# The second MoE's first product as fifteen block products on a Trainium2 core, with an order from a list scheduler

## The chip, the core and the metric

The kernel runs on one core of a Trainium2 chip. The metric is device time in microseconds (us) of one execution, and the median of three runs stands for the kernel. All weights, activations and results are float32. A product is made exact enough by splitting each operand in a high part of reduced precision (`hi`) and the rest (`lo`) and adding three TensorE products: hi·hi, hi·lo and lo·hi.

The engines are named as the profile names them: PE is TensorE's matmul stream and PEld its weight loads, DVE is VectorE, ACT is ScalarE, POOL is GpSimd, and SP is SyncE, whose queue issues every DMA of this kernel. PSUM has 8 banks of 128x512 float32. TensorE writes only there, and DVE or ACT must read a bank out before it can be filled anew.

## What is computed

Three stages follow each other; the output of one is the input of the next.

```
attention:  state = f[t] * state + k[t] v[t]^T ;  y[t] = q[t] . state      (4 x 8 heads, 768 steps, 48 wide)
first MoE:  h = x @ w_in ;  g = h * sigmoid(1.702 h) ;  x = g @ w_out      (3072 tokens, 384 -> 2048 -> 384)
second MoE: p = domain_probs / sum(domain_probs)
            out = sum over e of  p[:, e] * (relu(x @ w1[e]) @ w2[e])       (4 experts, 384 -> 1024 -> 384)
```

The change concerns `x @ w1[e]` and all that follows from computing it in another way.

## The kernel before

Activations lie transposed in SBUF: features on the 128 partitions, 512 tokens in a row. 3072 tokens make six token tiles `j` (NB = 6), 384 features make three partition tiles (KD = 3).

**Attention and first MoE.** Two parts of the program carry them. `startup` runs an order that is written out as a table (`ORDER`), with all attention of the first two token tiles and 40 steps of the first MoE. The steps after that are 64 steps of 512 tokens (16 blocks of hidden features for each of the token tiles 2 to 5). A step `s` has a product into a bank (L538, nine matmuls), a tanh on ACT (L544), a multiplication on DVE that reads the bank (L546), the split into hi on ACT (L326) and lo on DVE or POOL (L328), and, two steps later, the second product (L556, nine matmuls, into three banks). `at` and `chunk_at` hang the attention of the chunks 12 to 23 between the first 48 of these 64 steps; the framework's own scheduler orders that part, under the engines' in-order queues. The last 16 steps stand in written order.

**Second MoE.** The weights are eight units `u` (two for each expert), each with a 384x512 block of `w1` and a 512x384 block of `w2`. The loop runs over u, j and four blocks `ft` of 128 hidden features. `L3` makes the first product: three parts of the precision scheme times three feature tiles, nine matmuls of 512 columns into bank 3 or 4 (L626); DVE takes the relu and multiplies by the token's probability (L633), then ACT and DVE split the result. `L4`, two steps behind, makes the second product, nine matmuls into three of six banks (L664), and after four `ft` DVE adds the three banks to an accumulator in `arena` (L675). The last unit's last token tile is computed with tokens on the partitions (`L4_last`, L697, 384 columns) so that no transpose stands at the end. `at` places the loads and splits of the next unit's weights among the steps. POOL has no work in this stage.

For each unit and pair of token tiles the first product so takes 3 x 3 x 4 x 2 = 72 matmuls: per 256 hidden features and three token tiles, 2 x 3 blocks of output with three 128-wide inner products each are 18 block products of three matmuls.

**Names.** `R` are twenty 128x1536 tiles (the first MoE's weights and inputs, later the second MoE's), `G` eight split results, `RAW` (`cv` in the profile) six 128x512 tiles that `raw_tile` hands out in turn, `WIDE` three 128x1024 tiles, `ydram` the first MoE's output in DRAM, `ptd` the probabilities there.

## Time and profile before

| | us |
|---|---|
| median of 3 runs (1318.56, 1320.10, 1320.69) | 1320.1 |
| span of the profiled execution, first to last instruction | 1318.0 |
| span from the first product of the second MoE to its last matmul | 787.7 |
| PE busy in the span | 1287.3 |
| DVE, ACT, POOL busy | 734.9, 385.4, 167.6 |

The profiled execution has no time of its own besides its span; the median is 2.1 us longer than that span, which is what lies around the first and the last instruction and the spread of the runs.

The profile is read in four views. The page gives the busy time of each engine and the chain that ended last. The view of windows gives the same busy times, the granted clock of TensorE (1.00 is the upper of its two levels, 2.4 GHz) and the DMA engines' busy share for stretches that one names. The view of groups by line gives count, busy time and mean duration. The timeline gives single instructions, with the idle time before them and what ended it in brackets.

### The profile page before, as it was taken

Reading aid. Unit: us, or ns where it says so; the run is one execution under the profiler, and the core shown is the slowest. Engines: PE = TensorE matmul, PEld = TensorE weight load, DVE = VectorE, ACT = ScalarE, POOL = GpSimd, SP = SyncE. Lnnn points to the kernel's source line nnn. Section 1 sums busy time; section 2 is a strip of 40 time slices with the busy share of each in tenths; the row PEclk is TensorE's granted clock in tenths of the full one; section 3 lists DMA queues with packets and bytes.
Section 4 is the critical chain, followed back from the end, with each engine's and each line's share of the span. In section 5 each row is a group of like instructions: output and inputs, shape, how many; then the busy total and the mean of one; then the engine's idle time right before and its main releaser. Section 6 shows DMA issues by size and latency. Waiting matters only on the chain.

```text
span 1318.0 us, 18850 instructions
## 1 busy us (share of the span) xinstructions
PE 1287.3 (98%) x7734; PEld 1069.2 (81%) x7734; DVE 734.9 (56%) x1111; ACT 385.4 (29%) x691; POOL 167.6 (13%) x179
## 2 busy tenths in 40 slices
PE   5799999999999999999999999999999999999998
PEld 4698887888888888888888888888888888888887
DVE  7889747666565354455454454454454454454554
ACT  4666634333333343222121121121121121121111
POOL 5877422111110022000000000000000000000000
PEclk6899999999999999999999999999999999999999
DMA  6554323112120042420100100100100100100353
GB/s 181 171 157 135 100 73 105 42 52 77 27 71 21 7 139 89 120 80 33 48 25 24 48 24 25 48 25 25 48 25 24 49 24 24 48 25 16 48 97 75
DMA packets 75040, 81.63 MB, mean 62 GB/s; under 512 B 43104, under 2 KB 44224, under 8 KB 74944
## 3 DMA queue, kind: packets, MB, share of 16 engines
q1 hardware_dynamic: 74944, 80.34, 21.6%
q8 instruction: 62, 1.02, 0.3%
q14 instruction: 34, 0.28, 0.1%
HBM read 66.90 MB, written 13.42 MB: 61 GB/s over the span
## 4 chain that ended last, share of the span: by engine, by line
PE 95%; POOL 2%; DMA 1%; ACT 1%; issue 1%; DVE 0%; SPq 0%; POOLq 0%; ACTq 0%
PE bank L626 30%; PE bank L664 29%; PE bank L538 15%; PE bank L556 15%; PE bank L496 2%; PE bank L428 2%; PE bank L422 1%; PE bank L697 1%; DMA wide<-in_w_in 1%; POOL cv L87 0%; PE bank L457 0%; POOL arena L441 0%; POOL arena L419 0%; DMA arena<-in_qkf 0%; POOL g L328 0%
## 5 line engine op out<-in xcount | busy, mean ns | idle before, releaser
L626 PE MATMUL bank<-r,r 128*128 128x512 f32 x1728 | 423.0, 390 | 0.0
L664 PE MATMUL bank<-g,r 128*128 128x512 f32 x1692 | 414.1, 390 | 0.0
L626 PEld LDWEIGHTS bank<-r,r 128*128 128x128 f32 x1728 | 324.5, 188 | 67.1
L664 PEld LDWEIGHTS bank<-g,r 128*128 128x128 f32 x1692 | 317.8, 188 | 65.7
L326 ACT CAST g<-wide 128x512 fp32r<-128x512 f32 x192 | 119.3, 621 | 633.0 <-DVE wide L633 633.0
L633 DVE SCALAR_TENSOR_TENSOR wide<-bank,wide 128x512 f32<-128x512 f32 x192 | 132.6, 691 | 244.9 <-PE bank L626 244.5
L538 PE MATMUL bank<-r,r 128*128 128x512 f32 (+1 forms) x936 | 219.7, 380 | 2.9 <-DVE arena L546 2.1
L556 PE MATMUL bank<-g,r 128*128 128x512 f32 (+1 forms) x936 | 215.9, 375 | 0.0
L328 DVE TENSOR_TENSOR g<-wide,g 128x512 fp32r<-128x512 f32 x192 | 132.9, 692 | 142.9 <-ACT g L326 142.9
L538 PEld LDWEIGHTS bank<-r,r 128*128 128x128 f32 x936 | 165.4, 190 | 36.3 <-DVE arena L546 2.3
L556 PEld LDWEIGHTS bank<-g,r 128*128 128x128 f32 x936 | 166.5, 188 | 32.7 <-DVE cv L565 0.7
L546 DVE SCALAR_TENSOR_TENSOR arena<-arena,bank 128x512 f32<-128x512 f32 (+1 forms) x104 | 66.0, 636 | 88.3 <-ACT arena L544 88.0
L544 ACT ACTIVATE arena<-bank 128x512 f32<-128x512 f32 (+1 forms) x104 | 58.7, 564 | 129.8 <-PE bank L538 129.3
L328 DVE TENSOR_TENSOR g<-arena,g 128x512 fp32r<-128x512 f32 (+1 forms) x82 | 60.4, 736 | 37.9 <-ACT g L326 37.8
L326 ACT CAST g<-arena 128x512 fp32r<-128x512 f32 (+1 forms) x104 | 61.0, 588 | 69.6 <-DVE arena L546 69.4
L675 DVE TENSOR_TENSOR arena<-arena,bank 128x512 f32<-128x512 f32 x123 | 77.4, 678 | 0.0
L326 ACT CAST r<-cv 128x512 fp32r<-128x512 f32 x84 | 51.4, 616 | 4.8 <-POOL cv L87 3.5
L328 DVE TENSOR_TENSOR r<-cv,r 128x512 fp32r<-128x512 f32 x70 | 49.0, 704 | 0.5 <-ACT r L326 0.4
L428 PE MATMUL bank<-arena 48*128 48x128 f32 x384 | 30.8, 304 | 12.5 <-issue 5.9
L428 PEld LDWEIGHTS bank<-arena 48*128 48x128 f32 x384 | 25.8, 205 | 17.4 <-issue 9.6
L412 DVE TENSOR_TENSOR_SCAN arena<-arena,ends 128x512 f32<-128x512 f32 x24 | 35.5, 1481 | 0.2
L406 DVE TENSOR_TENSOR_SCAN arena<-arena,floor 128x512 f32<-128x512 f32 x24 | 31.7, 1320 | 1.7 <-POOL s_dec L470 0.4
(79 smaller groups left out, 623.5 us busy)
## 6 DMA issues: line engine op xcount, KB each, us to landing
wide<-ptd SPq DMA_DIRECT2D x48, 256.0 KB, 3.6
cv<-in_w SPq DMA_DIRECT2D x42, 256.0 KB, 4.0
arena<-in_qkf SPq DMA_DIRECT2D x48, 192.0 KB, 3.5
ydram<-cv SPq DMA_DIRECT2D x30, 256.0 KB, 2.2
cv<-ydram SPq DMA_DIRECT2D x30, 256.0 KB, 3.5
arena<-in_v SPq DMA_DIRECT2D x24, 256.0 KB, 3.5
wide<-in_w_in SPq DMA_DIRECT2D x12, 512.0 KB, 4.5
wide<-in_w_out SPq DMA_DIRECT2D x12, 512.0 KB, 3.9
```

What stands on the lines that cost most here:

```text
L326: nc.scalar.copy(out=hi, in_=src)
L328: eng.tensor_tensor(out=lo, in0=src, in1=hi.bitcast(F32), op=ALU.subtract)
L412: nc.vector.tensor_tensor_scan(back, back, ends[:, ::-1], 0.0, ALU.mult, ALU.max)
L428: nc.tensor.matmul(ab(c)[1 + r][:, 128 * p:128 * p + 128], t[64 * r:64 * r + D, 1, p], t[64 * r:64 * r + D, 2, p], start=True, stop=True,)
L538: nc.tensor.matmul(h, w[:, c0:c0 + 128], x[:, 512 * k + t0:512 * k + t0 + n], start=(i == 0), stop=(i == 8),)
L544: nc.scalar.activation(out=th, in_=h, func=ACTF.Tanh, scale=0.851)
L546: nc.vector.scalar_tensor_tensor(out=gf, in0=th, scalar=1.0, in1=h, op0=ALU.add, op1=ALU.mult)
L556: nc.tensor.matmul(bank[d][:, t0:t0 + n], w[:, c0:c0 + 128], g, start=(f == fs[0] and i == 0 and t0 == 0), stop=(f == fs[-1] and i == 2 an ...
L626: nc.tensor.matmul(h, w[:, c0:c0 + 128], y[:, 512 * k:512 * k + 512], start=(i == 0), stop=(i == 8),)
L633: nc.vector.scalar_tensor_tensor(out=gf, in0=h, scalar=0.0, in1=wide(NB * u + j, 0), op0=ALU.max, op1=ALU.mult)
L664: nc.tensor.matmul(cur[d], w[:, c0:c0 + 128], h, start=(ft == 0 and s == 0), stop=(ft == 3 and s == 2),)
L675: nc.vector.tensor_tensor(out=a, in0=a, in1=cur[d], op=ALU.add)
```

## The change

The three weight blocks of 128 input features by two halves of 256 hidden features, and the three token tiles, are treated as a product of a 2x3 by a 3x3 matrix of blocks. Instead of the 18 block products of the ordinary rule, the new kernel computes 15 products of sums of blocks, from which the six output blocks follow exactly by additions (`FORM_W`, `FORM_Y`, `FORM_H`: which blocks are summed on the weight side, on the token side, and where a product enters).

- `w_forms`, `w2_piece`: in the 48 steps of the first MoE between which attention hangs, each unit's `w1` is loaded, POOL makes 12 sums of blocks (128x256), ACT and DVE split 15 forms into hi and lo, and SP stores them in DRAM (`wfd`, 15 x 256 KB for each unit). `w2` is split too and stored (`w2d`). The six `RAW` tiles carry all of it.
- `second_moe` builds a list of tasks with engine, an assumed duration and the buffers that they read and write; `Plan.order` puts them into an order, engine by engine, always taking the task that can begin first. TensorE's own order is fixed by a number for each task (`place`). The list begins with the last 16 steps of the first MoE (`l_task`, `m_task`) and the token side's first forms.
- 32 rounds `n` follow, one for each half unit of 256 hidden features and each half of the tokens (three token tiles). A round has 15 products of three matmuls (`p_task`, L1076) in five chains; a chain's products add up in one bank, and after each product ACT or DVE reads the running sum out (L1089, L1093), so that the next product of that chain waits for that read. Relu and split follow on ACT (L1100) and DVE (L1101). Then come nine second products of six matmuls (`u_task`, L1116), each read by DVE with the probability (L1129) and added to the accumulator by POOL (L1131). The last two rounds use 12 products of 384 columns (`u_last`, L1166).
- The token side's 15 forms of the second half are made on POOL during the rounds 2 to 12 (`later_forms`), kept in DRAM (`yfd`) and split in rounds 14 and 15. The first half's output leaves after round 15.

```diff
-    def L3(u, j, ft):
-        for w, y in ((whi, yhi), (whi, ylo), (wlo, yhi)):
-            for k in range(KD):
-                nc.tensor.matmul(h, w[:, c0:c0 + 128], y[:, 512 * k:512 * k + 512], start=(i == 0), stop=(i == 8))
-        nc.vector.scalar_tensor_tensor(
-            out=gf, in0=h, scalar=0.0, in1=wide(NB * u + j, 0), op0=ALU.max, op1=ALU.mult
-        )
...
+CHAINS = [[3, 8, 14, 11, 12, 0], [13, 7, 10, 6, 1], [2], [5], [4, 9]]
+TURN = [3, 13, 8, 7, 2, 14, 5, 10, 11, 4, 6, 9, 12, 1, 0]
+U_START = 17.0
...
+        def form(r):
+            def go():
...
+                        nc.gpsimd.tensor_tensor(
+                            out=t, in0=have[a], in1=have[b], op=ALU.add if sg > 0 else ALU.subtract
+                        )
...
+                hl = raw_tile().rearrange("p (i l c) -> p i l c", i=2, l=2)
...
+                    nc.scalar.copy(out=hi, in_=fv)
+                    nc.vector.tensor_tensor(out=lo, in0=fv, in1=hl[:, :, 0], op=ALU.subtract)
...
+                nc.sync.dma_start(
+                    out=wfd[2 * u:2 * u + 2, g, :, 256 * q:256 * q + 256].rearrange("i p c -> p i c"),
...
+        def dma(nbytes, fns, reads=(), writes=(), after=()):
...
+            return P.task("SP", 0.1 * max(1, nbytes // 262144), go, reads, writes, after, late=2.2 + nbytes / 220e3)
...
+            P.task("POOL", pool, lambda: nc.gpsimd.tensor_tensor(
+                out=a.ap, in0=a.ap, in1=m.ap, op=ALU.add), [a, m], [a])
...
+        plan = second_moe()
+        done = plan.order()
         with tc.manual_schedule():
-            first_steps(e, len(steps) - early)
...
+            for t in done:
+                t.fn()
```

How the instructions stand now is shown at three places. The first is PE's queue in the second MoE. Before, a step of the first product (L626) and one of the second (L664) alternate, nine matmuls each; `bank` is the PSUM bank, after the arrow stand the streamed operand and the weights.

```order
L626 MATMUL bank3_98<-r2_65,r14_77 128x512 x3
L626 MATMUL bank3_98<-r3_66,r14_77 128x512 x3
L626 MATMUL bank3_98<-r2_65,r15_78 128x512 x3
L664 MATMUL bank5_100<-g4_87,r18_81 128x512
L664 MATMUL bank6_101<-g4_87,r18_81 128x512
L664 MATMUL bank7_102<-g4_87,r18_81 128x512
L664 MATMUL bank5_100<-g5_88,r18_81 128x512
L664 MATMUL bank6_101<-g5_88,r18_81 128x512
L664 MATMUL bank7_102<-g5_88,r18_81 128x512
```

Now, at the end of round 10, products of three matmuls (L1076) stand between second products of six (L1116):

```order
L1076 MATMUL bank6_101<-r9_72,r13_76 128x512 x3
L1076 MATMUL bank5_100<-r3_66,r13_76 128x512 x3
L1116 MATMUL bank0_95<-r14_77,r7_70 128x512
L1116 MATMUL bank0_95<-g3_86,r7_70 128x512
L1116 MATMUL bank0_95<-r14_77,r7_70 128x512
L1116 MATMUL bank0_95<-g5_88,r7_70 128x512
L1116 MATMUL bank0_95<-r14_77,r7_70 128x512
L1116 MATMUL bank0_95<-g3_86,r7_70 128x512
L1076 MATMUL bank6_101<-r10_73,r13_76 128x512
L1076 MATMUL bank6_101<-r11_74,r13_76 128x512
L1076 MATMUL bank6_101<-r10_73,r13_76 128x512
```

Bank 6 is filled, must be read out, and is filled again with three plus six matmuls in between.

The second place is DVE's queue in the same stage. Before, it alternates between the relu that reads a bank (L633) and the split (L328), with three additions (L675) every four steps:

```order
L675 TENSOR_TENSOR arena_91<-arena_91,bank5_100 128x512
L675 TENSOR_TENSOR arena_91<-arena_91,bank6_101 128x512
L675 TENSOR_TENSOR arena_91<-arena_91,bank7_102 128x512
L633 SCALAR_TENSOR_TENSOR wide0_92<-bank3_98,wide2_94 128x512
L328 TENSOR_TENSOR g5_88<-wide0_92,g4_87 128x512
L633 SCALAR_TENSOR_TENSOR wide1_93<-bank4_99,wide2_94 128x512
L328 TENSOR_TENSOR g7_90<-wide1_93,g6_89 128x512
```

Now, in round 10, with the read of bank 6 that the PE rows above wait for in the sixth row:

```order
L1093 TENSOR_TENSOR arena_91<-arena_91,bank5_100 128x512
L1129 TENSOR_TENSOR arena_91<-bank2_97,cv01_123 128x512
L1093 TENSOR_TENSOR arena_91<-arena_91,bank4_99 128x512
L1129 TENSOR_TENSOR arena_91<-bank1_96,cv02_124 128x512
L1101 SCALAR_TENSOR_TENSOR r19_82<-arena_91,g7_90 128x512
L1093 TENSOR_TENSOR arena_91<-arena_91,bank6_101 128x512
L1093 TENSOR_TENSOR wide0_92<-wide0_92,bank5_100 128x512
L1129 TENSOR_TENSOR arena_91<-bank0_95,cv02_124 128x512
L1101 SCALAR_TENSOR_TENSOR g0_83<-arena_91,r19_82 128x512
```

The reads of banks now stand behind splits (L1101) that read two operands from SBUF.

The third place is SP's queue in the first MoE. Before, it holds the loads of attention (L386, L388) and every sixteen steps three stores of results (L571):

```order
L388 DMA arena_91<-in_v 128x512
L386 DMA arena_91<-in_qkf 48x512 x2
L571 DMA ydram_106<-cv01_120 128x512
L571 DMA ydram_106<-cv02_121 128x512
L571 DMA ydram_106<-cv10_122 128x512
L386 DMA arena_91<-in_qkf 48x512 x2
L386 DMA arena_91<-in_qkf 48x1024 x2
```

Now the stores of the forms (L794), the loads of `w2` (L807) and the stores of its halves (L810, L811) stand between the same loads (L527, L529):

```order
L527 DMA arena_91<-in_qkf 48x512
L794 DMA wfd_109<-cv00_122 128x2x256
L794 DMA wfd_109<-cv10_125 128x2x256
L807 DMA cv11_126<-in_w2 128x512
L527 DMA arena_91<-in_qkf 48x1024 x2
L810 DMA w2d_110<-cv12_127 128x512
L811 DMA w2d_110<-cv11_126 128x512
L794 DMA wfd_109<-cv10_125 128x2x256
L807 DMA cv02_124<-in_w2 128x512
L529 DMA arena_91<-in_v 128x512
```

208 DMAs have come into this part of the queue: 16 loads of `w1`, 24 of `w2`, 120 stores of forms and 48 of the halves of `w2`.

## Rows read from the trace of the kernel before

**Rows 1.** The page: busy time by engine, and the chain that ended last.

```profile
PE 1287.3 (98%) x7734; PEld 1069.2 (81%) x7734; DVE 734.9 (56%) x1111; ACT 385.4 (29%) x691; POOL 167.6 (13%) x179
...
PE 95%; POOL 2%; DMA 1%; ACT 1%; issue 1%; DVE 0%; SPq 0%; POOLq 0%; ACTq 0%
```

**Rows 2.** Windows: stretch, length, busy us, PEclk, DMA share, GB/s.

```profile
182.00:456.00 274.00, 273.88 (x2453) 223.19 (x2453) 160.98 (x251) 101.12 (x185) 38.43 (x56) 1.00 0.19 55
100.00:140.00 40.00, 40.00 (x254) 33.84 (x253) 37.22 (x49) 27.54 (x52) 28.48 (x22) 1.00 0.42 130
523.80:1311.50 787.70, 787.70 (x3487) 653.95 (x3485) 396.50 (x602) 149.74 (x251) 0.00 (x0) 1.00 0.16 42
```

**Rows 3.** PE's timeline, second MoE's start and end: start, span, instruction.

```profile
531.95 2.20 PE L626 MATMUL bank<-r,r 128*128 128x512 f32 x9
...
536.03 2.20 PE L626 MATMUL bank<-r,r 128*128 128x512 f32 x9
...
1301.03 2.27 PE L697 MATMUL bank<-r,g 128*128 128x384 f32 x12
1303.13 2.24 PE L626 MATMUL bank<-r,r 128*128 128x512 f32 x9
```

**Rows 4.** Groups by line, PE, whole span: count, busy us, mean ns.

```profile
L626 PE MATMUL bank<-r,r 128*128 128x512 f32 x1728 | 423.0, 390 | 0.0
L664 PE MATMUL bank<-g,r 128*128 128x512 f32 x1692 | 414.1, 390 | 0.0
...
L697 PE MATMUL bank<-r,g 128*128 128x384 f32 x48 | 8.7, 336 | 0.0
```

**Rows 5.** Groups by line and form: DVE from 182 to 456 us.

```profile
L328 DVE TENSOR_TENSOR g<-arena,g 128x512 fp32r<-128x512 f32 x51 | 36.9, 724 | 24.8 <-ACT g L326 24.8
...
L412 DVE TENSOR_TENSOR_SCAN arena<-arena,ends 128x512 f32<-128x512 f32 x14 | 21.1, 1507 | 0.1
...
L406 DVE TENSOR_TENSOR_SCAN arena<-arena,floor 128x512 f32<-128x512 f32 x14 | 17.1, 1225 | 1.1
```

**Rows 6.** The same view, DVE and POOL, whole span.

```profile
L546 DVE SCALAR_TENSOR_TENSOR arena<-arena,bank 128x256 f32<-128x256 f32 x16 | 6.4, 408 | 2.5 <-ACT arena L544 2.5
...
L342 POOL TENSOR_TENSOR cv<-cv,cv 128x512 f32<-128x512 f32 x12 | 16.7, 1390 | 71.0 <-DMA cv<-ydram 70.6
...
L328 POOL TENSOR_TENSOR g<-arena,g 128x256 fp32r<-128x256 f32 x10 | 10.5, 1053 | 3.0 <-ACT g L326 3.0
```

**Rows 7.** Timeline of POOL and DVE around 329 and 75 us.

```profile
328.94 1.80 POOL L419 TENSOR_TENSOR arena<-arena 128x512 f32<-128x512 f32 x1 [7.36 <-DMA arena<-in_qkf]
329.51 1.79 DVE L328 TENSOR_TENSOR g<-arena,g 128x512 fp32r<-128x512 f32 x1
...
74.90 0.72 POOL L328 TENSOR_TENSOR g<-arena,g 128x256 fp32r<-128x256 f32 x1
```

**Rows 8.** DMA: two windows of 5 us, then issues with KB and us to landing.

```profile
180.00:185.00 5.00, 5.00 (x54) 3.89 (x53) 3.89 (x9) 2.90 (x7) 1.80 (x2) 1.00 0.66 213
535.00:540.00 5.00, 5.00 (x24) 4.14 (x23) 1.68 (x3) 1.21 (x2) 0.00 (x0) 1.00 0.94 268
...
ydram<-cv SPq DMA_DIRECT2D x30, 256.0 KB, 2.2
```

**Rows 9.** Timeline of one step of the first MoE.

```profile
332.90 2.20 PE L538 MATMUL bank<-r,r 128*128 128x512 f32 x9
...
335.20 0.60 ACT L544 ACTIVATE arena<-bank 128x512 f32<-128x512 f32 x1 [2.10 <-PE bank L538]
...
337.21 0.69 DVE L328 TENSOR_TENSOR g<-arena,g 128x512 fp32r<-128x512 f32 x1 [0.69 <-ACT g L326]
```

**Rows 10.** SP's queue: waits from 182 to 456 us, then two timeline rows.

```profile
SPq L386 <- PE bank L496: 120.6, 10, 17.6
...
194.93 1.31 SPq L571 DMA_DIRECT2D ydram<-cv  x3
1284.33 7.05 SPq L646 DMA_DIRECT2D out<-cv  x12
```

More of the change, by code (lines that the diff above doesn't have):

```diff
@@ new lines, with __init__, ap, at @@
+U_TOKENS = [2, 1, 0]
+U_START = 17.0
+LAST_U = 30
+class Buf:
+    def __init__(self, pool, parts=None):
+        self.pool, self.slot = pool, None
+        self.writers, self.readers, self.refs = [], [], []
+    @property
+    def ap(self):
+        return self.slot.ap
+class Slot:
+    def __init__(self, ap, free=0.0):
+        self.ap, self.held, self.free = ap, None, free
+    def at(self):
+        if self.held is None:
+            return self.free
+        if any(t.end is None for t in self.held.refs):
+            return None
+        return max([self.free] + [t.end + t.late for t in self.held.refs])
@@ L278, in attention_moe_moe2_kernel @@
     ptd = dram.tile([4, NT], F32, name="ptd")
-    otd = dram.tile([512, DM], F32, name="otd")
+    yfd = dram.tile([15, 128, 512], F32, name="yfd")
+    wfd = dram.tile([2 * NU, 5, 128, 768], F32, name="wfd")
+    w2d = dram.tile([NU, 2, 128, 1536], F32, name="w2d")
+    otd = dram.tile([NT // 2, DM], F32, name="otd")
     yrows = [[i for i, g in enumerate(SEGS) if g[0] == j] for j in range(2)]
@@ L359, in attention_moe_moe2_kernel @@
     last = NB - 1
-    ys = [wout[0], win[1], wout[1], win[2], wout[2], win[3]]
-    us = [(xs[1 - last % 2], win[0]), (wout[3], xs[last % 2])]
     def eng(kind, i):
@@ L585, in L2, with slot, asl @@
             sums_store(row, tiles)
-    onum = [0]
-    obanks = [5, 6, 7, 0, 1, 2]
-    def wide(i, n):
-        return WIDE[i % 3].bitcast(F32)[:, 512 * n:512 * n + 512]
+    def slot(i):
+        return [*(WIDE[n // 2].bitcast(F32)[:, 512 * (n % 2):512 * (n % 2) + 512] for n in range(6)),
+                *RAW, ends, floor][i]
+    def asl(i):
+        return arena[:, 512 * i:512 * i + 512]
     def pr_make():
@@ L679, in attention_moe_moe2_kernel @@
[L679 to L705 removed]
+    place_of = {r: i for i, r in enumerate(TURN)}
@@ L775, in startup @@
                 step(int(ev[1:]), ev[0])
+    e_last = len(steps) - early - 16
     if True:
@@ L797, in attention_moe_moe2_kernel @@
                 chunk_at(4 * j + 4 + i, max(0, 16 * (j - 2) + 4 * i - 2))
[L799 to L838 removed]
+        e = len(steps) - early - 16
+        at(e - 8, pr_make)
+        when = [i for i in range(1, e - 1) if i % 16 not in (0, 1)]
+        work = []
+        for u in range(NU):
+            load, forms = w_forms(u)
+            pieces = [w2_piece(u, n) for n in range(3)]
+            work.append([load])
+            for i in range(5):
+                work.append(forms[3 * i:3 * i + 3] + (pieces[i // 2:i // 2 + 1] if i % 2 == 0 else []))
+        for i, fns in enumerate(work):
+            for fn in fns:
+                at(when[i * len(when) // len(work)], fn)
+        for i in range(e):
+            for fn in side.pop(i, []):
+                fn()
+            L1(early + i)
+            if len(pend) > 2:
+                L2()
         nc.vector.tensor_reduce(
```

637 lines of the change are left out of this document (491 added, 146 removed), and 8 rows, old and new, of tables (FORM_H, FORM_Y).

## The prediction

> **What bounds the kernel now.** I read the page first: PE is busy 98% of the span, and the chain that ended last is PE for 95% of it [rows 1]. A busy PE is not yet a PE at its peak, so the windows come next: from 523.8 to 1311.5 us PE never idles, its granted clock is 1.00, and POOL does nothing [rows 2]. The timeline then gives the pace: two steps of nine matmuls take 536.03 - 531.95 = 4.08 us, 0.2267 us for a matmul of 512 columns [rows 3], for a step that fills one bank and one that changes banks at every matmul alike. The groups give the counts [rows 4]: 1728 + 1692 matmuls of 512 columns at 0.2267 are 775.3 us, and 48 of 384 columns at (1303.13 - 1301.03) / 12 = 0.175 are 8.4, together 783.7. With the 18 matmuls of the first MoE that lie in the same stretch (4.1) this is the 787.7 of the window. So the second MoE is bound by the number of its matmuls alone, and a matmul less is worth 0.2267 us as long as nothing else makes PE wait.
>
> The stretch from 182 to 456 us, where the new work on weights goes, is bound by PE in the same way, but its cover is thinner: PE 273.9 of 274, DVE 161.0, ACT 101.1, POOL 38.4, DMA share 0.19 [rows 2].
>
> **Matmuls, the gain.** The new order holds 1440 matmuls at L1076, 1620 at L1116 and 144 of 384 columns at L1166. That is 3060 x 0.2267 + 144 x 0.175 = 693.7 + 25.2 = 718.9 us against 783.7: 64.8 us less. The shapes are the old ones (128x128 weights, 512 columns), so the pace is taken over. That the fifteen products are really fifteen the order shows (32 rounds x 15 x 3 = 1440); the rival that the change does not do what it says is closed. The profiled execution spans 1318.0 us, the median is 1320.1; I add the 2.1 between them to every result, so with no new wait the median is 1318.0 - 64.8 + 2.1 = 1255.3.
>
> **First MoE's stretch, the largest cost.** Eight units bring 120 forms, 96 sums and 24 pieces of w2 into 274 us in which PE has no slack. Each resource in turn.
>
> DVE: 120 splits of 128x256. The nearest row, 128x256 with one operand in PSUM, is 0.408 [rows 6]: 49 us, so 210 of 274. ACT: 120 halves of 128x256 at less than the 0.60 of a 128x512 [rows 9] and 24 pieces at that are below 87 us, so 188 of 274. POOL: 96 sums at 0.72 (undisturbed [rows 7]) to 1.05 (mean [rows 6]) and 24 subtractions at 1.39 [rows 6] are 102 to 134, so 141 to 172 of 274.
>
> DVE and POOL are not independent. At 328.94 a POOL operation took 1.80 us, and beside it a DVE split of two SBUF operands took 1.79 [rows 7] instead of 0.69 [rows 9]. DVE's splits and scans with two SBUF operands in this stretch take 75 us now [rows 5], 124 with the new ones; with POOL's 141 they ask for 265 of 274 us if no part of them overlaps. In SBUF — State Buffer, section "SBUF: two separate sides", the Trainium skill says that DVE with two SBUF inputs and GpSimd take one port pair as a lock for the whole instruction: then nothing overlaps, which speaks against this change and is the mechanism of rival (b). The two rows at 329 us agree with it in kind; but from 100 to 140 us DVE and POOL were busy 37.2 and 28.5 of 40 us and PE lost nothing [rows 2].
>
> DMA: 6.3 MB of w1 and 6.3 of w2 are read, 12.6 of w2's halves and 31.5 of forms are written, 56.6 MB. Loads reached 268 GB/s at a share of 0.94 (285 if full); a window with three stores 213 at 0.66 (323 if full) [rows 8]. At the full rates the new traffic takes 44 + 137 = 181 us, if stores keep their pace with 1 KB rows, and 56.6 MB at 268 GB/s are 211; with the old 0.19 x 274 = 52 it is 233 to 263 of 274. In DMA: Bandwidth & Descriptors, section "Specifications", the Trainium skill gives about 358 GB/s as the HBM limit of a core; by that estimate the new traffic is 158 us, this item is slack, and of the 15 us below some 5 would go. No window here comes near that rate, so the measured one decides.
>
> So DVE, DMA and the pair stand at 77 to 97% of the stretch and none above 100%. Every queue is in order: an ACT cast that waits for one of six `cv` tiles, a store or a POOL sum holds the tanh behind it. What hides such a wait: a step's second product begins 4 x 2.04 = 8.2 us after its first has ended, and the chain of tanh, product and split takes 337.21 + 0.69 - 334.94 = 3.0 us [rows 9], so about 5 us of delay in one step cost nothing. The bounds: 0, since nothing exceeds the window (a gain is excluded, PE's work there is the same); and 265 / 0.85 - 274 = 38 if in-order queues fill the pair, or DMA, to 85% only. I take **15**, nearer to the row from 100 to 140, but not 0, because DMA stood at 0.42 there and stands near 0.9 here.
>
> **Hand-over, 16 steps.** At its head SP issues 21 loads of results, three of probabilities and the first weights, in the plan 0.1 us apart and landing 3.4 us later, so the last of the 21 after 6. The trace shows 1.31 / 3 = 0.44 us for an issue [rows 10] and 256 KB at 268 GB/s are 1 us, so it lands after about 25. Twelve POOL sums and eight DVE sums wait for these loads, and DVE's multiplications of the running steps (L877) stand behind. Between 0 (5 us are free in each step, and the first form is due only after 16 x 4.08 = 65 us) and 25 - 6 - 5 = 14; I take **3**.
>
> **Steady rounds.** A round is 99 x 0.2267 = 22.4 us of PE. DVE has 24 operations of 0.69, 16.6 us, POOL nine additions of 1.39 (the nearest row [rows 6]), 12.5, and ACT 11 of 0.6. Five splits of a round have two SBUF operands and meet POOL's additions half the time, which adds 5 x 0.5 x 0.7 = 1.7 to DVE: 18.3 of 22.4. The closest place is the bank-6 pair in the order: between its end and its next filling PE has 3 + 6 matmuls, 2.04 us. The read begins 335.20 - 334.94 = 0.26 after the end [rows 9], takes 0.69, and stands behind a split that on its own ends in time: about 0.9 us are spare. A POOL addition just begun holds that split for up to 1.39, which costs at most 0.5 once a round, 16 in 31 rounds, and at least 0; in the middle, where an addition is often not just begun, about 0.13 a round: **4**.
>
> **The turn at half and the end.** After round 15, 36 stores in 128-byte pieces leave. Twelve such stores kept SP for 7.05 us [rows 10], so 36 take 21 of the round's 22.4 us, and weights for the next round queue behind, which are asked for more than ten microseconds ahead. 0 to 8, I take **2**. The tail after the last matmul has the old form; 0.
>
> **Sum.** 1255.3 + 15 + 3 + 4 + 2 = 1279.3, say **1280**.
>
> **Rivals.** (a) All is hidden in the stretch. For it: each resource has room on average, and 100 to 140 us shows full queues without loss. Then only hand-over, rounds and turn cost up to 9: 1255 to 1265. (b) The port pair and DMA fill to 85% only, 38 us, and the rounds pay 10 rather than 4: 1255.3 + 38 + 3 + 10 + 2 = 1308, with 1298 to 1317 around it. For it: three loaded in-order queues that wait for each other; against it: the row from 100 to 140. (c) Slower: SP's one queue. Attention's loads hold it while they wait for PE, 120.6 us in ten waits, the longest 17.6 [rows 10]. Nothing urgent stands behind them today. Then 208 DMAs do, and while a load holds the queue no store leaves, the six `cv` tiles fill up, and ACT stops with its tanh. Price: 284 issues (76 are there before) at 0.44 are 125 us, the holds 121, and 24 loads of w2 that wait for the landing of their tile's last store (2.2 us [rows 8]) 53: 299, 25 more than the stretch. It makes the kernel slower once the sum passes 274 + 65 = 339, that is if the holds grow by 40 us; with 60 more it is 1255.3 + 85 + 9 = 1349. Against it: the order puts the loads among the stores, not ahead of them, so much of the holding should go.
>
> **How the numbers follow.** Forecast (stretch 5 to 30, 1266 to 1298): 0.55. (a): 0.20. (b): 0.16. Within the noise: 0.02. (c): 0.07. The range leaves out (c), the upper part of (b) and the lowest of (a): 1257 to 1311. About 0.2% (2.6 us) is what a measurement of this kernel can tell from no change. Faster by more 0.91, within 0.02, slower 0.07.
>
> **What will show it.** The gain: groups at L1076, L1116 and L1166 with 1440, 1620 and 144 matmuls, and 4.08 us for 18 in the rounds. The stretch: the time from the first cast of a form (L786) to the last of the 48 steps, 274 before, and PE's idle time there, put down to L679 or L697 behind ACT or DVE, with DMA shares near 0.9. Rival (c): SP's waits for PE, with casts that wait for stores. The rounds: PE idle at L1076 behind DVE L1093. Wrong would be a pace over 0.2267 us with a PE that never idles, or over 50 us of idle PE in the rounds. If PE idles for long at a time its clock may fall too, which my sum does not contain.

## The result, and the profile of the changed kernel

The changed kernel takes 1339.0 us, the kernel before 1320.4 (medians of four runs each, side by side): 1.015 times as long, 95% interval 1.0135 to 1.0166. I had forecast 1280. The profiled execution spans 1337.5 us; by the matmuls that are gone it should span 1318.0 - 64.8 = 1253.2, so 84.3 us were lost on the way.

The page of the changed kernel, busy time by engine and the chain that ended last (beside [rows 1]):

```profile
PE 1249.2 (93%) x7470; PEld 1026.9 (77%) x7470; DVE 975.6 (73%) x1443; ACT 515.5 (39%) x967; POOL 691.2 (52%) x591
...
PE 66%; DVE 11%; DMA 10%; issue 5%; POOL 5%; ACT 2%; SPq 1%; DVEq 0%; ACTq 0%; POOLq 0%
```

PE is busy for 38 us less, not 65, and it is 66% of the chain instead of 95%.

Groups by line, PE, whole span, and its timeline in a round (beside [rows 3, 4]):

```profile
L1076 PE MATMUL bank<-r,r 128*128 128x512 f32 x1440 | 376.9, 391 | 9.9 <-DVE arena L1093 8.2 <-DVE wide L1093 1.1 <-ACT arena L1089 0.3
L1116 PE MATMUL bank<-r,r 128*128 128x512 f32 x876 | 273.9, 389 | 0.0
L1116 PE MATMUL bank<-g,r 128*128 128x512 f32 x744 | 242.9, 389 | 0.0
```

```profile
701.06 1.52 PE L1076 MATMUL bank<-r,r 128*128 128x512 f32 x6
...
705.14 0.61 PE L1116 MATMUL bank<-g,r 128*128 128x512 f32 x2
```

The counts are those of the sum (L1166 has its 144 in two further groups, 76 and 68), and 6 + 2 + 2 + 2 + 6 = 18 matmuls take 705.14 - 701.06 = 4.08 us, as before. The gain of 64.8 us is there.

Where the 84 us went, by windows (length, busy us, PEclk, DMA share, GB/s). The borders are the first matmul of step 49, where the last sixteen steps of the first MoE begin (L869, 515.9 us), and the first matmul of the second MoE (L1076, 592.6):

```profile
182.00:515.90 333.90, 292.51 (x2433) 232.38 (x2433) 231.64 (x376) 151.59 (x331) 148.74 (x170) 0.95 0.67 212
515.90:592.60 76.70, 70.01 (x290) 55.37 (x289) 51.41 (x63) 27.57 (x49) 30.98 (x21) 0.96 0.41 144
605.00:936.00 331.00, 330.90 (x1457) 273.31 (x1458) 250.42 (x359) 102.63 (x170) 196.69 (x139) 1.00 0.52 166
936.00:990.00 54.00, 49.80 (x212) 38.95 (x211) 48.75 (x73) 19.07 (x33) 21.87 (x15) 1.00 0.78 188
990.00:1285.00 295.00, 295.00 (x1303) 244.21 (x1302) 220.60 (x321) 87.94 (x144) 161.38 (x115) 1.00 0.44 133
1285.00:1296.00 11.00, 5.79 (x19) 4.31 (x18) 5.89 (x9) 2.42 (x4) 2.27 (x2) 0.69 0.69 130
```

The same two stages before:

```profile
182.00:458.40 276.40, 276.28 (x2465) 225.08 (x2465) 161.67 (x252) 102.27 (x187) 38.43 (x56) 1.00 0.19 55
458.40:523.80 65.40, 65.40 (x292) 54.20 (x291) 30.86 (x45) 26.89 (x48) 16.68 (x12) 1.00 0.36 118
```

- The stretch with the work on weights: step 49 begins at 515.9 instead of 458.4, **57.5 us**. PE is idle for 333.9 - 292.5 = 41.4 of them, and the same work keeps it busy for 292.5 instead of 276.3 us, some 16 more, at a granted clock of 0.95 instead of 1.00.
- The hand-over: 76.7 - 65.4 = **11.3**.
- In the rounds PE is idle for 0.1 us from 605 to 936 and not at all from 990 to 1285. The turn at half and the end of round 29 lose 6 and 7 (each matmul's start against the pace of 0.2267), the first round 1.3.

57.5 + 11.3 + 1.3 + 6 + 7 is 83; the rest lies at the start and in the tail.

**How one pause comes about.** The longest in the stretch, before 383.9, in the timeline of all engines (start, length, instruction; in brackets the idle time before it and what ended it):

```profile
364.68 0.56 SPq L758 DMA_DIRECT2D wide<-in_w  x1
...
369.83 2.31 POOL L777 TENSOR_TENSOR wide<-wide 128x256 f32<-128x256 f32 x3 [6.88 <-DMA wide<-in_w]
...
377.99 0.62 POOL L538 TENSOR_SCALAR arena<-arena 128x512 f32<-128x512 f32 x1
...
378.64 0.47 DVE L543 TENSOR_SCALAR floor<-arena 128x4 f32<-128x4 f32 x1 [1.89 <-POOL arena L538]
...
379.12 0.71 ACT L616 COPY s_bd<-s_dec 64x192 f32<-64x192 f32 x2 [2.09 <-POOL s_dec L611]
379.22 2.17 DVE L547 TENSOR_TENSOR_SCAN arena<-arena,floor 128x512 f32<-128x512 f32 x1
...
380.17 0.59 ACT L685 ACTIVATE arena<-bank 128x512 f32<-128x512 f32 x1
...
383.18 0.67 DVE L687 SCALAR_TENSOR_TENSOR arena<-arena,bank 128x512 f32<-128x512 f32 x1
...
383.91 3.80 PE L679 MATMUL bank<-r,r 128*128 128x512 f32 x9 [5.88 <-DVE arena L687]
387.54 2.23 PE L697 MATMUL bank<-g,r 128*128 128x512 f32 x9
```

Read it from the bottom. PE waits 5.88 us for DVE's product (L687), which stands in its queue behind attention's scan (L547, 2.17 us here, 1.22 on average in [rows 5]) and two splits of forms that follow it. The scan stands behind a floor (L543) that waits for attention's gate on POOL (L538), and the gate stands behind ten sums of weight blocks on POOL, 369.8 to 378.0. The product's other input, the tanh on ACT (L685), is late by the same sums: it stands behind a copy (L616) that waits for another step of attention on POOL (L611). The first sum waited 6.88 us, for a load issued at 364.7. After the pause PE's nine matmuls take 387.54 - 383.91 = 3.63 us instead of 2.04:

```profile
384.00:387.00 3.00, 3.00 (x7) 2.38 (x8) 3.00 (x6) 1.61 (x4) 1.51 (x1) 0.50 0.36 126
```

The granted clock of these 3 us is 0.50, the lower level of 1.2 GHz. So a pause costs more than its length.

### The profile page after: what moved, and what is told of

Read it like the earlier page. It is cut to its first block, busy times and chain, and to the rows that moved or that the text cites. A ratio compares the mean times of both kernels' runs of the same rounds, so it can differ in the third digit from the quotient of the medians.

```text
span 1337.5 us, 20734 instructions
## 1 busy us (share of the span) xinstructions
PE 1249.2 (93%) x7470; PEld 1026.9 (77%) x7470; DVE 975.6 (73%) x1443; ACT 515.5 (39%) x967; POOL 691.2 (52%) x591
## 4 chain that ended last, share of the span: by engine, by line
PE 66%; DVE 11%; DMA 10%; issue 5%; POOL 5%; ACT 2%; SPq 1%; DVEq 0%; ACTq 0%; POOLq 0%
PE bank L1116 25%; PE bank L1076 23%; PE bank L697 6%; PE bank L679 5%; DMA wfd<-cv 3%; PE bank L1166 2%; POOL wide L777 2%; PE bank L893 1%; PE bank L637 1%; DMA cv<-in_w 1%; DVE cv L787 1%; DVE arena L553 1%; DMA w2d<-cv 1%; PE bank L569 1%; DVE r L938 1%
## 5 line engine op out<-in xcount | busy, mean ns | idle before, releaser
L1131 POOL TENSOR_TENSOR arena<-arena 128x512 f32<-128x512 f32 x252 | 358.9, 1428 | 270.9 <-DVE arena L1129 270.3
L1076 PE MATMUL bank<-r,r 128*128 128x512 f32 x1440 | 376.9, 391 | 9.9 <-DVE arena L1093 8.2
L1076 PEld LDWEIGHTS bank<-r,r 128*128 128x128 f32 x1440 | 269.9, 188 | 69.9 <-DVE arena L1093 11.9
L1116 PE MATMUL bank<-r,r 128*128 128x512 f32 x876 | 273.9, 389 | 0.0
L1129 DVE TENSOR_TENSOR arena<-bank,cv 128x512 f32<-128x512 f32 x252 | 173.2, 688 | 112.4 <-PE bank L1116 106.7
L1116 PE MATMUL bank<-g,r 128*128 128x512 f32 x744 | 242.9, 389 | 0.0
L1116 PEld LDWEIGHTS bank<-r,r 128*128 128x128 f32 x876 | 164.7, 188 | 34.4
L679 PEld LDWEIGHTS bank<-r,r 128*128 128x128 f32 x792 | 140.8, 194 | 52.4 <-DVE arena L687 22.8
L697 PEld LDWEIGHTS bank<-g,r 128*128 128x128 f32 x774 | 138.5, 193 | 37.4 <-ACT cv L708 6.0
L1116 PEld LDWEIGHTS bank<-g,r 128*128 128x128 f32 x744 | 139.8, 188 | 29.1
L1093 DVE TENSOR_TENSOR arena<-arena,bank 128x512 f32<-128x512 f32 x192 | 130.1, 683 | 31.4 <-ACT arena L1089 22.8
L1089 ACT ACTIVATE arena<-bank 128x512 f32<-128x512 f32 x101 | 60.4, 598 | 108.6 <-PE bank L1076 107.8
L1100 ACT ACTIVATE r<-arena 128x512 fp32r<-128x512 f32 x75 | 47.1, 632 | 131.7 <-DVE arena L1093 131.7
L777 POOL TENSOR_TENSOR wide<-wide 128x256 f32<-128x256 f32 x64 | 54.9, 874 | 59.0 <-DMA wide<-in_w 33.4
L687 DVE SCALAR_TENSOR_TENSOR arena<-arena,bank 128x512 f32<-128x512 f32 (+1 forms) x88 | 54.9, 626 | 33.1 <-ACT arena L685 30.9
L1093 DVE TENSOR_TENSOR wide<-wide,bank 128x512 f32<-128x512 f32 x96 | 65.6, 683 | 17.7 <-ACT wide L1089 12.2
L471 DVE TENSOR_TENSOR g<-arena,g 128x512 fp32r<-128x512 f32 (+1 forms) x66 | 57.5, 871 | 22.9 <-ACT g L469 22.2
L787 DVE TENSOR_TENSOR cv<-wide,cv 128x256 f32<-128x256 f32 x72 | 41.4, 584 | 33.3 <-ACT cv L786 33.1
```

Source lines behind the costliest of these rows:

```text
L471: eng.tensor_tensor(out=lo, in0=src, in1=hi.bitcast(F32), op=ALU.subtract)
L679: nc.tensor.matmul(h, w[:, c0:c0 + 128], x[:, 512 * k + t0:512 * k + t0 + n], start=(i == 0), stop=(i == 8),)
L687: nc.vector.scalar_tensor_tensor(out=gf, in0=th, scalar=1.0, in1=h, op0=ALU.add, op1=ALU.mult)
L697: nc.tensor.matmul(bank[d][:, t0:t0 + n], w[:, c0:c0 + 128], g, start=(f == fs[0] and i == 0 and t0 == 0), stop=(f == fs[-1] and i == 2 an ...
L777: nc.gpsimd.tensor_tensor(out=t, in0=have[a], in1=have[b], op=ALU.add if sg > 0 else ALU.subtract)
L787: nc.vector.tensor_tensor(out=lo, in0=fv, in1=hl[:, :, 0], op=ALU.subtract)
```

## Experiments

Four explanations stood for trial. L: once in a unit, everything hangs on one chain, the load into the only buffer, the sums, the casts in ACT's queue. P: DVE and POOL hold each other up at a common port. R: the ring of six tiles is too short, and casts wait for stores. Q, formed later: POOL's queue, in order, with attention's steps behind the work on weights. The measure is the start of step 49, 458.4 before and 515.9 in the changed kernel, from one profile each. Two of the kernels below, e7 and e12, are the same program up to there, and in them it begins at 472.7 and 474.7; four runs of e12 lie up to 7.6 us apart in total. Differences of a few us are therefore read with caution.

**E1 to E3: loads, sums, half of the work.**

```diff
 e1  +  if u: load = lambda: None
 e2  +  src = src if src < 6 else src % 6
 e3  -  for u in range(NU):                  wfd[n % 16, g]   divmod(n % 16, 2)
     +  for u in range(NU // 2):             wfd[n % 8, g]    divmod(n % 8, 2)
```

> The changed kernel, but w1 is loaded for the first of the eight units only (2 of 16 loads, 5.5 MB less to read); the forms of all units are made from it, so the weights of seven units are left out of the result. Measure: the start of the first matmul of step 49 (515.9 us in the changed kernel; 458.4 where the kernel before does the same step), and the total (1339). Theory L (once in a unit everything hangs on one chain: the load into the only buffer, the first POOL sums, the cast in ACT's queue with the tanh behind it): POOL no longer waits 33 us for loads, step 49 begins at 475 to 490, total 1300 to 1315. Rival P (DVE and POOL fill their common port, or DMA is full): a tenth of the new DMA traffic goes, the port is as full as before: 508 to 514, total 1331 to 1337. Rival R (the ring of six tiles is too short for casts that wait for stores): nothing that a tile waits for changes: 512 to 517.

> The changed kernel without the 96 POOL sums of weight blocks: the twelve forms of a unit that need a sum are made from one block each, so the sums are left out of the result; 120 casts, 120 splits and all DMAs stay. Start of step 49, 515.9 in the changed kernel: theory L expects 490 to 500, since casts wait for the load itself and only the 3 to 4 us of sums behind it go, in eight units; total 1315 to 1323. Rival P: the demand on the port falls from 265 to about 182 of 274 us, and nearly all of the 57 us goes: 460 to 470, total 1285 to 1293. Rival R: 510 to 517, total 1334 to 1340.

> The changed kernel with the forms and the halves of w2 of four units instead of eight, spread over the same steps; the second MoE reads them twice, so the weights of the other four units are left out of the result. Every count of new operations and bytes in the stretch is halved. Start of step 49, 515.9 in the changed kernel: theory L expects about half of the 57 us, 480 to 492, as four units have four chains; total 1303 to 1315. Rivals P and R, where a resource is too full, expect almost nothing of it to be left, since every share falls to 60% and below: 458 to 466, total 1281 to 1289.

The last sixteen steps' first products (first and last start at the end) in e1, e2, e3:

```profile
L869 PE MATMUL bank<-r,r x144: 387/389/473, 490.7 to 555.9; 128*128 128x512 f32 x144
```

```profile
L870 PE MATMUL bank<-r,r x144: 387/389/628, 485.0 to 554.8; 128*128 128x512 f32 x144
```

```profile
L869 PE MATMUL bank<-r,r x144: 387/389/473, 474.1 to 538.7; 128*128 128x512 f32 x144
```

Loads give 25.2 of 57.5 us back (just past the edge of what L said), sums 30.9 (more than L, less than P), half of the units 41.8: half of the work costs 15.7, less than half and not nothing. In e3's stretch DVE is busy 194 of 292 us, POOL 101, and the DMA share is 0.52; nothing there but PE is near full, and PE still pauses. No single theory fits, and the parts overlap: 25 + 31 and the 28 of e6 are more than 57.

**E4 and E8: loads earlier.** One group is left empty behind a unit's load, and the 15 forms stand in four groups instead of five (e4 on the changed kernel, e8 on e7). In e4 a tile of the ring that holds a piece of w2 can be overwritten before it is used, so that part of the result is changed.

```diff
-  for i in range(5):
-      work.append(forms[3 * i:3 * i + 3] + ...)
+  work.append([])
+  for i in range(4):
+      work.append(forms[4 * i:4 * i + 4] + ...)
```

> The changed kernel with the same operations, but every load of a unit stands one group (5.7 us) further ahead of its first form, and the load of a piece of w2 one group ahead of its cast; the 15 forms of a unit then stand in four groups of 4, 4, 4 and 3 instead of five of 3. Start of step 49, 515.9 in the changed kernel: theory L expects 475 to 495, total 1298 to 1318, as loads have landed before the engine asks for them. Rival P: no change, 513 to 519. Rival R: no change or later, since a piece of w2 holds its tile longer: 515 to 530.

> e7 with each unit's load one group further ahead of its first form, the 15 forms in four groups of 4, 4, 4 and 3. Theory L (the load that lands late is what is left): 458 to 468, total 1276 to 1290. If the denser groups cost as much as the earlier load gives, as e4 (515.9 against 517.4) hints: no earlier than e7.

Step 49 at 517.4 (changed kernel 515.9) and 474.8 (e7 472.7): nothing gained in either. Whether an earlier load gives something that the denser groups take again, these two don't show.

**E5 to E7: the work moved.** These compute everything. e5 makes the sums on DVE (gpsimd becomes vector in that one call). e6 takes w2 out of the stretch: each round loads its half of w2 as it is, into the two tiles of the pool T (Y in rounds 16 and 17), and splits it. e7 is both.

```diff
-  nc.gpsimd.tensor_tensor(out=t, in0=have[a], in1=have[b], ...)
+  nc.vector.tensor_tensor(out=t, in0=have[a], in1=have[b], ...)
...
-  dma(786432, go, (), [b], after)
+  for f in range(2):
+      x = Buf("Y" if n in (16, 17) else "T")
+      dma(196608, lambda x=x, f=f: [(x.ap[:, 0:384], w2[u]...[:, f, i])], (), [x], after)
+      P.task("ACT", 0.5, <copy x to the high half of b>, [x], [b])
+      P.task("DVE", 0.56, <x minus it to the low half of b>, [x, b], [b])
```

> The changed kernel with the 96 sums of weight blocks on DVE instead of POOL (a 128x256 operation takes 0.41 to 0.43 us there, 0.86 on POOL); nothing else is changed. Start of step 49, 515.9 in the changed kernel, 485.0 with the sums left out: if the sums cost by their length and by the hop from POOL to ACT (theory L), about two thirds of the 31 us that their absence gave come back, less what 39 us more of DVE cost: 495 to 505. If they cost by sharing the port with DVE (rival P), DVE's splits get short and nearly all of the 31 us come back: 485 to 493. If DVE is now the engine that is late: 516 to 525.

> The changed kernel, but w2 is taken out of the first MoE's stretch: its 24 loads, 24 casts, 24 POOL subtractions and 48 stores there are gone, and each of the 32 rounds loads its half of w2 as it is and splits it (two ACT casts and two DVE subtractions of 128x384). In the stretch this takes away 48 of 180 uses of the six tiles, those held longest, and 18.9 of 56.6 MB. Start of step 49, 515.9 in the changed kernel: rival R, 475 to 490; rival P (DMA, port), 488 to 500; theory L alone (w1's chain is as before), 505 to 513. The rounds get 1.1 us more of DVE and 1.0 more of ACT out of 22.4 each: 740 us from the end of the first MoE to the last matmul, and 0 to 6 more. Total 1300 to 1340.

> e6 and e5 together: w2 split in the rounds, the sums of weight blocks on DVE; POOL has no work on weights left in the stretch. If the two costs are separate, the gains add up: start of step 49 at 465 to 485 and a total of 1285 to 1305. If both had only removed the same wait, it stands no earlier than the better of the two alone.

The same row of e5, e6 and e7, and e7's window of the stretch:

```profile
L869 PE MATMUL bank<-r,r x144: 387/389/473, 496.6 to 568.3; 128*128 128x512 f32 x144
```

```profile
L869 PE MATMUL bank<-r,r x144: 387/389/474, 488.2 to 552.7; 128*128 128x512 f32 x144
```

```profile
L869 PE MATMUL bank<-r,r x144: 387/389/473, 472.7 to 537.3; 128*128 128x512 f32 x144
```

```profile
182.00:472.70 290.70, 281.58 (x2471) 227.83 (x2470) 231.42 (x469) 141.27 (x308) 45.34 (x60) 0.99 0.61 198
```

19.3 us from the sums (where L had it), 27.7 from w2 (at the border of R and P), 43.2 from both: nearly additive. Totals: 1316.2, 1307.7 and 1290.8 beside a kernel before of 1319.9. In e7 DVE is busy 80% of the stretch, against 69% in the changed kernel (231.6 of 333.9), and PE loses 14 us instead of 57; so a full DVE is not what cost the time. With e6 the hand-over is down to 64.5 us for the same sixteen first products (74.5 in the changed kernel, 515.9 to 590.4).

**E9, E13, E14, E17: why POOL's sums cost 31 us.** In all four the forms are made from one block each, and the sums are made and never read; their sort differs.

```diff
 e9   -  f = have[src]
      +  f = have[src if src < 6 else src % 6]
 e13  +  e9, and in0=R[0].bitcast(F32)[:, 0:256], in1=R[0].bitcast(F32)[:, 256:512]
 e14  +  e9, and out=t[:, 0:8], in0=have[a][:, 0:8], in1=have[b][:, 0:8]
 e17  +  e14, and for _ in range(2): nc.gpsimd.memset(t, 0.0)
```

> The changed kernel with all 96 POOL sums made, but no cast reads them: every form is made from one block, so the sums are left out of the result. POOL does the same work at the port, and nothing waits for its sums any more except the next unit's load. Start of step 49, 515.9 in the changed kernel, 485.0 without the sums. Rival P (the sums cost by holding DVE up at the common port): 508 to 516, total 1331 to 1339. Theory L (they cost because casts in ACT's queue wait for them): 483 to 492, total 1301 to 1311. In between, the share of each can be read off: every us above 485 is the port's.

> e9 (96 sums on POOL that nobody reads; forms made from one block each), but each sum adds two blocks that lie in SBUF all the time, so that POOL does the same work in the same order and waits for no load. Start of step 49: e9 524.4, e2 without sums 485.0. Rival P (the port): 508 to 524, total 1331 to 1346. Theory Q (POOL's queue stands still at a sum whose load hasn't landed, and attention's steps on POOL behind it hold DVE and ACT): 485 to 497, total 1302 to 1314.

> e9, but each sum adds only the first 8 of the 256 columns of its two blocks: POOL waits for the same loads in the same order, and occupies the port hardly at all. The sums are unread, as in e9. Start of step 49: e9 524.4, e2 485.0. Theory Q: 505 to 522, total 1327 to 1344. Rival P: 485 to 495, total 1302 to 1312. If it lies between, both have a share, and e13 and e14 should then add up to e9's 39 us.

> e14 (sums of 8 columns that nobody reads; forms made from one block each), with two fills of the sum's 128x256 tile behind each, some 0.3 us each, so that POOL's queue is occupied for about as long as by the sums of e9 but reads nothing. Start of step 49: e9 524.4, e14 490.2. If occupation of POOL's queue is the cost: 510 to 524, total 1331 to 1346. If it is the port that DVE and POOL share in two-operand work: 488 to 497, total 1309 to 1318, with DVE's splits of 128x256 at the 0.44 to 0.49 us of e14 and e2 rather than e9's 0.66.

Windows up to step 49 of e9, e14 and e17 (the fifth busy time is POOL's), and DVE's group of the forms' splits, whole span, in the same order (e17's line stands two lower):

```profile
182.00:524.40 342.40, 299.87 (x2491) 238.63 (x2489) 230.00 (x379) 152.89 (x332) 143.93 (x166) 0.94 0.64 208
```

```profile
L787 DVE TENSOR_TENSOR cv<-wide,cv 128x256 f32<-128x256 f32 x72 | 46.1, 657 | 26.7 <-ACT cv L786 26.3 <-DMA wfd<-cv 0.2
```

```profile
182.00:490.20 308.20, 282.00 (x2433) 225.75 (x2431) 211.82 (x377) 151.41 (x331) 92.67 (x164) 0.98 0.71 230
```

```profile
L787 DVE TENSOR_TENSOR cv<-wide,cv 128x256 f32<-128x256 f32 x72 | 33.9, 486 | 29.5 <-ACT cv L786 27.4 <-DMA wfd<-cv 1.8
```

```profile
182.00:497.00 315.00, 284.76 (x2431) 226.90 (x2431) 212.21 (x377) 152.82 (x332) 138.04 (x332) 0.98 0.69 226
```

```profile
L789 DVE TENSOR_TENSOR cv<-wide,cv 128x256 f32<-128x256 f32 x72 | 32.3, 463 | 27.1 <-ACT cv L788 26.8
```

Where nobody reads the sums, step 49 begins at 524.4, later than with readers (and later than the 508 to 516 of rival P): the cost does not need casts that wait for sums, which theory L had from the waits. e14 lies 5.2 us above e2, so the waits for loads in POOL's queue make that much at most, as P expected. e17, with POOL busy for 138 us, nearly e9's 144, adds 6.8 and ends at the upper edge of what was expected of the port. The other 27.4 of e9's 524.4 - 485.0 = 39.4 us come only with sums of full length that read two SBUF operands.

The port is at work there: the splits of 128x256 on DVE take 0.657 us on average in e9, 0.486 in e14 and 0.463 in e17. In e9, 31 of these 72 splits (L787) have no POOL operation beside them and take 0.42 us each; the 40 beside a two-operand operation of POOL take 0.85 on average, up to 1.50. In e17 the 15 beside a fill take 0.42. DVE's product with one operand in PSUM (L687) does not get longer beside POOL in e9: 0.66 us, and 0.68 without. Over the stretch DVE is busy for 230.0 us in e9 and 212.2 in e17.

But e9 and e17 also differ in the order on POOL, and that is a rival which no run excludes. With no readers a sum waits for no free tile, and the twelve sums of a unit move together into a train. In e9, ahead of its longest pause, attention's gate (L538) stands behind all twelve, 9.9 us after the start of the first; in e17 it stands behind eight of them, 5.9 us after the start of the first. The same place in e9 and e17:

```profile
408.45 3.83 POOL L777 TENSOR_TENSOR wide<-wide 128x256 f32<-128x256 f32 x4
...
418.36 0.62 POOL L538 TENSOR_SCALAR arena<-arena 128x512 f32<-128x512 f32 x1
...
418.42 0.71 ACT L616 COPY s_bd<-s_dec 64x192 f32<-64x192 f32 x2 [8.21 <-POOL s_dec L611]
...
421.64 4.21 PE L679 MATMUL bank<-r,r 128*128 128x512 f32 x9 [9.31 <-DVE arena L687]
```

```profile
390.03 1.00 POOL L777 TENSOR_TENSOR wide<-wide 128x8 f32<-128x8 f32 x2
...
395.96 0.62 POOL L538 TENSOR_SCALAR arena<-arena 128x512 f32<-128x512 f32 x1
...
398.75 3.64 PE L679 MATMUL bank<-r,r 128*128 128x512 f32 x9 [4.78 <-DVE arena L687]
```

That is theory Q: what the main chain needs of POOL stands behind a train of sums, as behind the ten sums of the pause shown above. The port makes a train longer, but how the 27.4 us divide between the port and POOL's order is not shown. Part of the loss comes through the clock: of the 34.2 us between e14 and e9, 16.3 are more idle time of PE (42.5 against 26.2) and about 6 lie ahead of 182 us, where a train already held up a step (the next step's first product starts at 177.0 in e9 and at 170.8 in e14); the rest, a good third, is PE at a lower granted clock, 0.94 against 0.98.

In SBUF — State Buffer, section "SBUF: two separate sides", the Trainium skill says that a DVE instruction with two SBUF inputs is kept out only by a GpSimd operation that reads SBUF. The fills of e17, which read nothing, agree: 0.42 us for a split beside one.

e13 failed as a test of the port: step 49 begins at 537.6, later than either side expected. Its sums waited for nothing, and all of them stand at the head of POOL's queue:

```profile
192.76 1.26 POOL L471 TENSOR_TENSOR g<-arena,g 128x512 fp32r<-128x512 f32 x1
193.98 11.70 POOL L777 TENSOR_TENSOR wide<-r 128x256 f32<-128x256 f32 x17
205.64 1.26 POOL L471 TENSOR_TENSOR g<-arena,g 128x512 fp32r<-128x512 f32 x1
```

POOL's splits of the first MoE's steps stood behind trains of 17 sums, 11.7 us each, and where the kernel before stood at 203 us PE was 51 us late. So a train does cost when a step's own split stands behind it; it is theory Q with a price, from trains longer than the ten sums in the changed kernel's longest pause.

**E10, E11, E15: the ring and w2.** e10 and e11 leave the sums out as e2 does and use their 6 KB: for three more tiles of the ring, or for the pieces of w2, loaded one group ahead. e15 is the changed kernel with w2's subtraction on DVE.

```diff
 e10  -  return RAW[raw_n[0] % 6]
      +  return RING[raw_n[0] % len(RING)]      # 9 tiles
 e11  -  r, h = raw_tile(), raw_tile()
      +  r, h = <one of three tiles of its own, loaded a group ahead>, raw_tile()
 e15  -  nc.gpsimd.tensor_tensor(out=r, in0=r, in1=h, op=ALU.subtract)
      +  nc.vector.tensor_tensor(out=r, in0=r, in1=h, op=ALU.subtract)
```

> e2 (no sums, their part of the result left out) with the 6 KB of the sums' tiles given to the ring: nine tiles instead of six. Start of step 49, 485.0 in e2. Rival R (casts wait for stores of the tile's last use): half or more of the 26.6 us that are left go, 465 to 473, total 1283 to 1291. If the ring was long enough and the loads of w1 and w2 are what is left: 482 to 487, total 1300 to 1306.

> e2 (no sums, their part of the result left out) with the 6 KB of the sums' tiles used for the pieces of w2 as they are loaded, so that each is asked for one group (5.7 us) ahead of its cast, and takes one tile of the ring instead of two. Start of step 49, 485.0 in e2. If w2 cost 28 us (e6) because its cast in ACT's queue stands behind a load that has just been asked for: 470 to 478, total 1288 to 1296. If it cost by bytes or by POOL's subtractions at the port, which are all still there: 482 to 487.

> The changed kernel with the 24 subtractions of w2 on DVE instead of POOL; sums stay on POOL. In the changed kernel POOL waits 59.7 us at them for ACT's cast. Start of step 49, 515.9 in the changed kernel, 488.2 with w2 out of the stretch altogether (e6). Theory Q: half or more of these 28 us come from POOL's queue, 492 to 503, total 1314 to 1326. If w2 costs by its tiles, bytes and ACT's casts: 508 to 517, total 1331 to 1340.

Step 49 at 472.0, 480.5 and 507.6. The ring is worth 13.0 us of the 26.6 that e2 left, in the range of R; ACT's waits for stores in e2 show where:

```profile
ACT cv L787 <- DMA wfd<-cv: 12.3, 12, 2.0
ACT cv L790 <- DMA w2d<-cv: 10.8, 11, 2.0
ACT cv L790 <- DMA wfd<-cv: 9.8, 11, 2.1
```

w2's loads asked for earlier give 4.5, between what the two sides expected, and its subtractions off POOL 8.3, well short of theory Q's 13 to 24 and just past the other side's 8. How the rest of w2's 27.7 divides among tiles, stores, casts and bytes was not separated.

**E12, E16, E18: a kernel faster than both.** e12 is e7 with the plan's prices for SP's issues and output tiles taken from the trace, and with round 18's piece of w2 also in a tile of the pool Y. e16 is e7 with the forms that need no sum first, and with outputs of round 29 also in tiles of the pool Y. e18 is e16 with four tiles for sums and seven in the ring.

```diff
 e12  -  P.task("SP", 0.1 * max(1, nbytes // 262144), go, ..., late=2.2 + nbytes / 220e3)
      +  P.task("SP", cost or 0.35, go, ..., late=2.2 + nbytes / 220e3 + (2.5 if cost else 0.0))
      +  kept[t, d] = dma(262144, store, [r], cost=2.3)
 e16  +  first = [6, 7, 14, 3, 8, 13]
      +  r = Buf("Y" if n != 15 and d == 1 else "T")
 e18  +  half[made[0] % 4], and a seventh tile in the ring
```

> e7 (w2 split in the rounds, sums on DVE) with the plan's prices taken from the trace: 0.35 us of SP for a DMA instead of 0.1, and for an output tile that leaves in four DMAs 2.3 us and a landing 2.5 us later. In e7 PE loses 11 us around the turn at half (880 to 972) and 6.7 near the end (1255 to 1273), where DVE's transposes wait for one of two tiles still being stored and hold the reads of PE's banks. If that wait is the cause, the list scheduler now puts the transposes later and 6 to 14 us go: 1277 to 1285 against 1290.8. If the two tiles are the limit whatever the order is: 1288 to 1294.

> e7 (w2 split in the rounds, sums on DVE), the three forms of a unit that need no sum made first, while DVE makes the sums of the others, and a third tile or two for the outputs that leave near the end. e7: start of step 49 at 472.7, 6.7 us of PE lost between 1255 and 1273, total 1290.8. If ACT's 22 us of waiting for DVE's sums are part of what is left: 460 to 469; if two tiles are what the end lacks, 3 to 6 us less there. Total with both 1277 to 1286, with one 1284 to 1289, with neither 1289 to 1294.

> e16 with four tiles for sums instead of six, and the 2 KB so freed as a seventh tile of the ring. Start of step 49: 470.4 in e16, 458.4 where nothing is added to the stretch. If casts that wait for a tile's last store are most of what is left: 459 to 466, total 1277 to 1285. If DVE's sums or the loads are: 468 to 475, total 1286 to 1293.

Against the kernel before: e12 1291.8 us, ratio 0.9775 (0.9752 to 0.9798); e16 1290.5, 0.9784 (0.9768 to 0.98); e18 1286.6, 0.9749 (0.9731 to 0.9768). All three are faster than both kernels, by 2.2 to 2.5% than the one before; the three are hardly told apart, e12's own runs reach from 1286.3 to 1293.9. e12 is no faster than e7's 1290.8: it loses some 6 us instead of 11 around the turn, but 8 instead of 7 near the end. More output tiles (e16) brought the loss there from 6.7 to 3.7 us; with the forms that need no sum made first, step 49 begins at 470.4, not at the 460 to 469 that were expected. The seventh tile didn't move step 49 (473.1 against 470.4); as e18 also took two tiles from the sums, that does not show that the ring has room with w2 gone. What still costs 12 to 15 us before step 49 was not found.

## Why the prediction was wrong, step by step

- **Matmuls, -64.8.** Right: counts and pace as written.
- **The stretch, 15 of 0 to 38.** Measured 57.5, above the upper bound. This is the step that failed, in three places. First, its bounds compared sums of busy time with the window, as if a stretch lost nothing until a resource is full. The sums themselves came out near: DVE 231.6 us against 210, POOL 148.7 against 141 to 172, ACT 151.6 against 188, DMA 0.67 x 333.9 = 224 against 233 to 263. But e3, with DMA at 0.52 and every engine but PE below 70%, loses 15.7, and e7, with DVE fuller than ever, 14.3. Second, the nearest row that I chose, 100 to 140 us with no loss [rows 2], is a stretch ordered by hand, whose waits end in time; here the scheduler set the order (that a hand order would have lost less, no run shows). Third, the 5 us of cover for a step assumed one delay at a time, where the pause shown above strings together a load of 5 us, ten sums, a gate, a scan and a product. POOL's in-order queue, with attention's steps behind the sums, stands nowhere in the sum. The two rows at 329 us [rows 7] had shown the port rightly, and I priced it as capacity; what it costs as a delay on a chain is open, as port and POOL's order together make the 27 us by which e9 exceeds e17.
- **PE's clock.** I named it and left it out of the sum. Some 16 of the 57.5 us are at the lower level.
- **Hand-over, 3 of 0 to 14.** 11.3, within the bounds. The mechanism was the one named, SP's queue, at another place: three stores of results stood behind the loads, and DVE's product waited 8.80 us for the tile to come free:

```profile
530.23 1.68 SPq L847 DMA_DIRECT2D ydram<-arena  x3
...
536.94 0.69 DVE L877 SCALAR_TENSOR_TENSOR arena<-arena,bank 128x512 f32<-128x512 f32 x1 [8.80 <-DMA ydram<-arena]
```

- **Steady rounds, 4 of 0 to 16.** 0.1 us from 605 to 936. POOL's additions and DVE's splits meet there too, but nothing is late.
- **The turn, 2 of 0 to 8.** 6, within the bounds, but by luck: none of PE's pauses there waits for weights behind the stores on SP. Each ends with a read of a bank on DVE (L1093), and DVE, which also splits the second half's forms there, is busy for 48.8 of the 54 us. **The end, 0.** 7: round 29 sends out tiles in the same way as round 15, and I did not count them. A transpose on DVE waits for one of two tiles to be stored, and reads of PE's banks stand behind it:

```profile
1290.11 0.71 DVE L1135 STREAM_TRANSPOSE ends<-arena 128x512 f32<-128x512 f32 x1 [5.26 <-DMA otd<-ends]
1290.74 0.65 DVE L1093 TENSOR_TENSOR arena<-arena,bank 128x512 f32<-128x512 f32 x1
```

- **Rivals.** (c) gave 1349, near the 1339, by luck: the holds that it prices didn't occur. SP's holds at attention's loads fell from 120.6 us [rows 10] to 7.7 behind the same matmuls; SP waits instead for the engines whose results it stores:

```profile
SPq L794 <- DVE cv L787: 70.8, 42, 7.5
...
SPq L527 <- PE bank L637: 7.7, 2, 7.4
```

(b) named the port, which the splits of e9 show at work, but as a full resource, and its 38 us were too few. None of my cases had many short chains through all queues, with the clock on top.

## What to carry to other kernels

When side work is put into a stretch where PE just never waits, ask for each in-order queue what stands behind the new work and how late its inputs can land; busy shares far below 100% don't make it free, and here half of the work still cost 16 us. Add the clock to every pause of PE, which here made 41 idle us cost 57. Place side work where the pace has slack, as the rounds had for w2. The engine with more idle time is not always the better one: the sums cost 19.3 us less on DVE than on POOL (e5), though DVE was the fuller of the two.

## What the hardware showed that I had not expected

- DMA moved 336 GB/s in one window at a share of 0.92, more than the 268 of [rows 8] and than the 285 and 323 that I worked out from those rows as full rates:

```profile
520.00:540.00 20.00, 16.20 (x69) 12.63 (x67) 7.98 (x10) 4.74 (x9) 9.60 (x8) 0.93 0.92 336
```

- A two-operand sum of 128x256 on POOL takes 0.69 us in a train by itself (11.70 / 17 in e13) and 0.87 among DVE's splits in e9 (the mean of 48), while POOL's fills left DVE's splits at 0.46.
